# Gate products with the values as the stationary operand, logits by token rows, in an attention and mixture-of-experts kernel

## The chip, the cores and the metric

The kernel runs on one core of one Trainium2 chip. The metric is the device time of one execution in microseconds (us), the median of several runs of the whole kernel. Engines are named as in the profile: PE (TensorE, the matrix engine; PEld are its loads of a stationary operand), DVE (VectorE), ACT (ScalarE), POOL (GpSimd) and SP (the engine whose queue issues most transfers).

## The reference

Attention with a threshold over 8 batches of 8 heads (576 tokens, head size 64), then a router that gives every token to one of 8 experts with a fixed capacity of 576 tokens, then each expert's two-layer network. The change concerns one line of it, the gate product `logits = x @ w_gate`.

```python
scores = q @ k.T / 8                                  # each of 8 x 8 heads, 576 x 576
scores = where(scores >= max(scores) - tau, scores, -1e9)
attn = exp(scores - max(scores)); attn /= sum(attn) + 1e-9
x = (attn @ v), heads side by side                    # 4608 tokens x 512
logits = x @ w_gate                                   # 4608 x 8
# all 4608 * 8 logits in falling order: a token goes to the first expert that still has room
out[tokens of e] = relu(x[tokens of e] @ w1[e]) @ w2[e]
```

## The kernel before

The program has two stages. Attention for all batches comes first; the router and the experts come behind it. The change lies in the attention stage and its last few microseconds.

**Tiles and passes.** A batch has 4 pairs of heads, a pair has 9 tiles of score rows (eight of 128 rows, and the last, number 8, with the remaining 64 rows of both heads), so there are 288 tiles. The main loop at the end of `attention` takes two tiles a pass, 144 passes, 18 to a batch. A tile goes through several passes: its scores on PE (`score`, L69), in the next passes the negated minimum and a copy on DVE (`mx`, L74), the threshold on POOL (L75), the exponential on ACT (`ex`, L86), the masked product with its row sum on DVE (`stt`, L90), eight transposes of 64x64 pieces on PE (`tr`, through `turn`, L98) and their eviction by ACT (`trev`, L116 and L118). The products with the values (`pv_unit`, L155, and `pl_unit`, L165, for the last 64 keys) stand in a list, `queue`, with due passes, and `columns` takes from it. Their outputs collect in two PSUM banks (`xo`, one for columns 0 to 255 of the tokens and one for 256 to 575), are evicted by ACT at L145 and form `XT[b]`: for each of the four head pairs a tile of 128 partitions (two heads of 64) by 576 tokens, not yet divided by the row sums. `RD[b]` holds the reciprocals of the sums, `Lg` the logits by token rows.

**Order.** Every engine works in the order in which the program is written. In one pass PE gets: scores of two tiles, the transposes of leftover pieces where a tile 8 is near (`left`; such passes are called p8, four of every nine), what `columns` takes, one unit from `side` unless the pass is p8, and the transposes of two older tiles. Evictions noted in `later` are issued by ACT in the next pass (`flush`).

**The score tile.** A tile of scores uses columns 0 to 287 of two PSUM banks. Columns 288 to 511 are free; `free(t)` gives them to other work, the leftover transposes and the side units.

**The gate.** When the last product of a batch is evicted, `finish(b)` appends two units to `aux` and two to the front of `side`. Those of `aux` run in the next two passes, also in p8 ones, when the second `xo` bank is free (`whole`): `lg_unit` multiplies with the gate weights as the stationary operand (L177: four head pairs, 128x32, in four column strips of the array, moving the 256 or 320 token columns of `XT`), and ACT evicts the result into `LT` (L179). Those of `side` run in the next passes that are not p8: `lgt_unit` transposes three, then two, blocks of 128 token columns of `LT` (L202 through `turn`, L98, in the timeline `sc<-ident,lt`), ACT evicts them into `lw` (L219), and POOL multiplies with the reciprocals and adds up heads (L223 to L231). The second of them also copies the reciprocals of the last 64 tokens across partitions (`both`, L185 on PE, L188 on ACT). The last 64 tokens of an even and of the following odd batch share a column of `Lg`; an odd batch puts them into partitions 64 to 127.

For batches 0 and 1 `side` then holds ten units of row transposes of `XT` (`xt_early`), which end in stores of rows to memory; later batches do these behind the loop. The last batch does its gate work in `tail`, behind the loop: `lg_mm` and `lg_ev` for both column ranges, `lgt_mm`, and the sums on DVE (`logits`, L208 and L210), which the router needs first.

The two places where a pass takes its units:

```python
if sc_: columns(); whole()
ready=[x for x in side if x[0]()]
if ready and not p8: side.remove(ready[0]); ready[0][1](sc_[-1])
```

Of the kernel before, what the change touches and what calls it, by code (L numbers as in the profile page):

```python
# [19 lines left out]
PPB=8; LTB=1; VTB=4; HOLD=1; XW=520; NBO=2; NDEF=4; XTB=4; XTY=1.05; XT0=2.0; XRB=2  # L20


def attention(ctx, tc, qk, vl, tau, wgd, xrows, xts, Lg, nb_batches, ident, dup, R, after_first):
# [143 lines left out]
    RD={}  # L167
# [4 lines left out]
    LT={}; lt6=cst.tile([128,D],F32,name="lt6")  # L172
    def lg_mm(b,f,ps):
        if f==0: LT[b]=wk.tile([128,S+D],F32,name="lt",bufs=LTB)
        q=FQ[f]; n=q.stop-q.start
        for j in range(4):
            T.matmul(ps[32*j:32*j+32,:n],wg[:,j],XT[b][:,j,q],start=True,stop=True,tile_position=(0,32*j))  # L177
    def lg_ev(b,f,ps):
        q=FQ[f]; n=q.stop-q.start; c=0 if f else HEAD(b); A.activation(LT[b][:,c:c+n],ps[:,:n],AF.Copy)  # L179
    def HEAD(b): return S-256+(D if b==nb_batches-1 else 0)  # L180
# [9 lines left out]
    def lg_unit(b,f):  # L190
        ps=bank_v([128,512],1)
        lg_mm(b,f,ps)
        def ev():
            lg_ev(b,f,ps)
            if f==1:
                if b==nb_batches-2: G.tensor_scalar(lt6,LT[b][:,256:320],1.0,0.0,op0=ALU.mult,op1=ALU.add)
                have["lt"]=b
        return ev
    def lgt_mm(b,c0,c1,ps):
        for c in range(c0,c1):  # L200
            a=HEAD(b)+128*c if c<2 else 128*c-256 if c<4 else 192 if b%2 and b<nb_batches-1 else 256
            turn(ps[:,:,64*(c-c0):64*(c-c0)+64],LT[b][:,a:a+128])  # L202
    def lgt_in(ps,n): return ps[:,:,0:64*n].rearrange("p r (m k) -> p r m k",k=32)[:,:,:,0:16]
    def logits(b,c0,c1,ps,o):
        n=c1-c0; w=wk.tile([128,320],F32,name="lw",bufs=1)[:,0:64*n].rearrange("p (c j r h e) -> p c j r h e",c=n,j=2,r=2,h=2)
        lv=lgt_in(ps,n)
        for r in range(2):
            V.tensor_tensor(w[:,:,:,r].rearrange("p c j h e -> p (c j) h e"),lv[:,r].rearrange("p m (h e) -> p m h e",h=2),  # L208
                RD[b][:,r,c0:c1].rearrange("p c j h -> p (c j) h").unsqueeze(3).to_broadcast([128,2*n,2,8]),op=ALU.mult)
        V.tensor_reduce(Lg[:,o:o+n,:],w.rearrange("p c j r h e -> p c e (j r h)"),axis=AX.X,op=ALU.add)  # L210
    LW={}
    def lgt_unit(b,half,t):
        n=5 if b<nb_batches-2 else 4
        c0,c1=((0,3),(3,n))[half]; y=free(t)
        lgt_mm(b,c0,c1,y)
        if half: both(b,y[:,:,128:])
        else: LW[b]=wk.tile([128,320],F32,name="lw",bufs=1).rearrange("p (r c j h e) -> p r c j h e",r=2,c=5,j=2,h=2)
        w=LW[b]
        A.activation(w[:,:,c0:c1].rearrange("p r c j h e -> p r (c j) (h e)"),lgt_in(y,c1-c0),AF.Copy)  # L219
        if half: both_ev(b,y[:,:,128:],slice(0,128),A)  # L220
        for r in range(2):
            v=w[:,r,c0:c1].rearrange("p c j h e -> p (c j h) e")
            G.tensor_tensor(v,v,RD[b][:,r,c0:c1].rearrange("p c j h -> p (c j h)").unsqueeze(2).to_broadcast([128,4*(c1-c0),8]),op=ALU.mult)  # L223
        v=w[:,:,c0:c1]
        G.tensor_tensor(v[:,0],v[:,0],v[:,1],op=ALU.add)
        G.tensor_tensor(v[:,0,:,0],v[:,0,:,0],v[:,0,:,1],op=ALU.add)
        m=min(c1,4)-c0
        G.tensor_tensor(Lg[:,4*b+c0:4*b+c0+m,:],v[:,0,0:m,0,0],v[:,0,0:m,0,1],op=ALU.add)
        if c1==5:
            r=slice(64*(b%2),64*(b%2)+64)  # L230
            G.tensor_tensor(Lg[r,28+b//2,:],w[r,0,4,0,0],w[r,0,4,0,1],op=ALU.add)  # L231
    XR={}
    def xt_early(b,c,i,t):
# [5 lines left out]
        if i==0: G.tensor_scalar(xr[:n,512:XW].rearrange("p (r k) -> p r k",r=2),RD[b][:n,:,c].rearrange("p r j h -> p r (j h)"),1.0,0.0,op0=ALU.mult,op1=ALU.add)  # L239
# [103 lines left out]
    for s_ in range(-2,NT//2-2):  # L343
# [16 lines left out]
        for t in sc_: mx(t)  # L360
# [653 lines left out]
```

## Time and profile before

| | |
|---|---|
| median of 3 runs | 979.26 us (976.64 to 979.54) |
| the profiled execution | 973.59 us, its span 971.8 us |
| attention stage, main loop | from 5.5 us to about 439 us of the span |
| granted PE clock | 0.990 of full speed over the span |
| PE, gate products L177 | 128 records, 418 ns mean, 11.4 us busy in all |
| PE, transposes of logits | 78 records, 243 ns mean, 5.8 us busy in all |
| ACT, evictions L179 and L219 | 16 and 14, 6.3 and 4.1 us |
| POOL, L223 to L231 | 76 operations, 23.7 us |

In rows of the profile `out<-in` are the program's names of tiles, then come partitions x elements and the count. A PE row has the part of the array that it uses (rows*columns) ahead of the operand. Busy time of a group is the union of its records; records of PE overlap, so the mean of one record is longer than its share. A window `a:b` is a stretch of the span in us.

### The profile page before, as it was taken

To read this page: it belongs to the slowest core of one execution; us is meant where nothing else is said; L and a number is where in the kernel's file an instruction comes from. 1 tells how busy PE (TensorE), PEld (TensorE's weight loads), DVE (VectorE), ACT (ScalarE), POOL (GpSimd) and SP (SyncE) were. 2 spreads that over 40 slices of the span, in tenths; PEclk is the share of its full clock that TensorE was granted. 3 is DMA by queue.
4 is the path that set the end of the run, shared out by engine and by line. 5 is a ranking of instruction groups with operands and counts; after the bars stand their busy time and mean duration, and the time that the engine had idled before them with its cause. 6 is when DMAs were issued, how large, how long until landed. Compare 5 with 4: busy or idle time off the path is not lost.

```text
span 971.8 us, 24280 instructions
## 1 busy us (share of the span) xinstructions
PE 943.4 (97%) x9235; PEld 704.5 (72%) x9235; DVE 764.0 (79%) x2086; ACT 639.3 (66%) x1297; POOL 279.8 (29%) x493
## 2 busy tenths in 40 slices
PE   7999999999999999998789999999999999999996
PEld 4566656566566665565678797897978979898994
DVE  8999999999999999996679888586887786535220
ACT  6999999999999999996554344342543425445330
POOL 2435354353434343340110403222203022310202
PEclk9999999999999999999889999999999999999998
DMA  7332253533432333206742525151524344431101
GB/s 257 103 119 88 85 184 102 200 129 110 168 116 93 123 110 113 87 2 226 263 131 95 173 98 154 56 187 58 178 79 142 120 138 140 137 120 38 39 12 44
DMA packets 35860, 117.01 MB, mean 120 GB/s; under 512 B 4384, under 2 KB 5024, under 8 KB 35232
## 3 DMA queue, kind: packets, MB, share of 16 engines
q1 hardware_dynamic: 28352, 92.85, 27.8%
q0 software_dynamic: 5888, 19.03, 6.3%
q10 hardware_dynamic: 1504, 3.59, 1.2%
q8 instruction: 73, 1.20, 0.5%
q14 instruction: 43, 0.35, 0.1%
HBM read 93.01 MB, written 21.38 MB: 118 GB/s over the span
## 4 chain that ended last, share of the span: by engine, by line
PE 89%; DVE 5%; DMA 3%; issue 2%; ACT 1%; POOLq 0%; SPq 0%; ACTq 0%; DVEq 0%
PE pf L844 22%; PE pf L876 20%; PE sc L69 15%; PE xo L155 14%; PE tb L98 8%; PE sc L98 2%; PE pt L789 2%; PE xo L165 2%; DVE pp L90 1%; PE rps L497 1%; DVE z L74 1%; DVE cmp L426 1%; PE xo L177 1%; PE xo L246 1%; DMA out_dram<-y,idx 1%
## 5 line engine op out<-in xcount | busy, mean ns | idle before, releaser
L74 DVE TENSOR_SCALAR_CACHE_REDUCE z<-sc 128x576 f32<-128x576 f32 x288 | 206.1, 752 | 16.9 <-PE sc L69 15.0
L75 POOL TENSOR_SCALAR nb<-nb,taub 128x1 f32<-128x1 f32 x288 | 144.9, 504 | 249.9 <-DVE z L74 187.3
L86 ACT ACTIVATE pp<-z,nb 128x576 f32<-128x576 f32 x256 | 193.1, 773 | 26.0 <-DVE z L74 22.7
L90 DVE SCALAR_TENSOR_TENSOR pp<-z,nb,pp 128x576 f32<-128x576 f32 x256 | 200.0, 813 | 0.0
L876 PE MATMUL pf<-w2h,H 128*128 128x512 f32 x576 | 193.9, 401 | 0.8 <-DVE H L426 0.8
L69 PE MATMUL sc<-qk 64*128 64x288 f32 (+1 forms) x1280 | 179.9, 426 | 0.9 <-DMA qk<-qk_dram 0.4
L155 PE MATMUL xo<-pt,vt 128*64 128x320 f32 (+1 forms) x1024 | 155.9, 420 | 0.0
L116 ACT ACTIVATE pt<-tb 128x512 f32<-128x512 f32 x253 | 137.5, 590 | 2.0 <-PE tb L98 1.4
L883 POOL DMA_INDIRECT out_dram<-y,idx x40 | 44.6, 1114 | 307.2 <-ACT y L879 198.3
L876 PE MATMUL pf<-w2l,H 128*128 128x512 f32 x320 | 128.9, 403 | 0.0
L876 PEld LDWEIGHTS pf<-w2h,H 128*128 128x128 f32 x576 | 106.5, 188 | 20.3 <-DVE H L426 1.3
L69 PEld LDWEIGHTS sc<-qk 64*128 64x128 f32 (+1 forms) x1280 | 94.3, 179 | 28.7 <-DVE z L74 4.0
L844 PE MATMUL pf<-xh,w1h 128*128 128x288 f32 (+2 forms) x512 | 110.3, 301 | 0.7 <-ACT xh L790 0.7
L844 PE MATMUL pf<-xl,w1h 128*128 128x288 f32 (+2 forms) x512 | 110.4, 302 | 0.0
L844 PE MATMUL pf<-xh,w1l 128*128 128x288 f32 (+2 forms) x512 | 109.5, 299 | 0.0
L879 ACT ACTIVATE y<-pf 128x512 f32<-128x512 f32 x40 | 23.9, 598 | 128.8 <-PE pf L876 127.5
L98 PEld LDWEIGHTS tb<-ident,pp 64*128 64x128 f32 x2032 | 75.2, 139 | 44.7 <-issue 18.9
L155 PEld LDWEIGHTS xo<-pt,vt 128*64 128x64 f32 x1024 | 60.7, 136 | 58.5 <-issue 32.4
L856 ACT ACTIVATE hf<-pf 128x576 f32<-128x576 f32 x56 | 36.5, 652 | 89.3 <-PE pf L844 82.5
L98 PE MATMUL tb<-ident,pp 64*128 64x64 f32 x2032 | 91.8, 227 | 3.3 <-ACT pt L116 3.0
L844 PEld LDWEIGHTS pf<-xh,w1h 128*128 128x128 f32 x512 | 82.1, 190 | 1.6 <-ACT xh L790 1.1
L844 PEld LDWEIGHTS pf<-xh,w1l 128*128 128x128 f32 x512 | 81.9, 189 | 0.1
(197 smaller groups left out, 1334.7 us busy)
## 6 DMA issues: line engine op xcount, KB each, us to landing
qk<-qk_dram SPq DMA_DIRECT2D x31, 864.0 KB, 4.6
vt<-vl_dram SPq DMA_DIRECT2D x32, 576.0 KB, 4.0
w2s<-w_dram SPq DMA_DIRECT2D x32, 512.0 KB, 4.9
w1s<-w_dram SPq DMA_DIRECT2D x28, 512.0 KB, 5.3
xrows<-pp SPq DMA_DIRECT2D x24, 260.0 KB, 2.4
xts<-xt SPq DMA_DIRECT2D x2, 1152.0 KB, 5.4
pt<-xts SPq DMA_DIRECT2D x2, 1152.0 KB, 5.2
xrows<-xr SPq DMA_DIRECT2D x8, 260.0 KB, 2.5
```

The costliest lines, as they stand in the source:

```text
L69: T.matmul(sc[o,f,:HS], kd["q",h][r,c], kd["k",h][r,:],start=True,stop=True)
L74: V.tensor_scalar(z,SC.pop(t)[:,:,:HS],-0.125,None,op0=ALU.mult,op1=ALU.min,accum_out=nb[:,0:1])
L75: G.tensor_scalar(nb[:,1:2],nb[:,0:1],taub[:,0:1],None,op0=ALU.add)
L86: A.activation(pview(t),ZB[t].rearrange("p a b -> p (a b)"),AF.Exp,bias=NBI[t][:,0:1],scale=-1.0)
L90: V.scalar_tensor_tensor(pv,ZB.pop(t).rearrange("p a b -> p (a b)"),NBI[t][:,1:2],pv,op0=ALU.is_le,op1=ALU.mult,accum_out=den_of(p)[:,p%4/ ...
L98: g=slice(64*r,64*r+64); T.transpose(o[:,r],x[r%len(x)][g],ident[g,g])
L116: else: A.activation(o,tb,AF.Copy)
L155: T.matmul(xo[64*h:64*h+64,:q.stop-q.start],v[:,f,128*u+64*h:128*u+64*h+64],PT[p][:,h,u,q],start=new,stop=last,skip_group_check=True)
L844: T.matmul(ps[:,h,:n],s[w][:,k,f*128:(f+1)*128],s[x][:,k,cols[h]],start=(i==0),stop=(i==11))
L856: A.activation(hf,ps[:,:,:HS],AF.Relu)
L876: T.matmul(ps[:,0,:],H[:,f,c:c+128],s[w][:,f],start=(f==0 and j==0),stop=e)
L883: G.indirect_dma_start(out=out,out_offset=IOA(ap=s["idx"][:n,t:t+1],axis=0),in_=y[:n],in_offset=None)
```

## The change

The stationary and the moving operand of the gate product change places. A 128x64 piece of `XT` (one head pair, 64 tokens) is loaded, and the 16 gate columns of that pair move through it: the result has tokens in partitions and is what the transposes made before. Two such pieces, for the lower and the upper 64 tokens of a chunk of 128, use the two column halves of the array. The gate units no longer use an `xo` bank, `LT`, `lg_unit`, `lgt_unit` and `whole` go, and a batch has three units in `side`: chunks 0 and 1, chunks 2 and 3, chunk 4 with `both`. POOL's operations of these units and the small copies of `xt_early` go into a list, `small`, from which each pass issues two; a row store first issues all that are left. In the tail the two products of the last batch become `gate(b,0,2,z)` and `gate(b,2,5,x)`.

```diff
+    def gate(b,c0,c1,ps):
         for c in range(c0,c1):
+            for j in range(4):
+                for a in range(2):
+                    x,q=(b,128*c+64*a) if c<4 else (b-a*(b==nb_batches-1),512)
+                    o=32*(c-c0)+16*(j%2)
+                    T.matmul(ps[64*a:64*a+64,j//2,o:o+16],XT[x][:,j,q:q+64],wg[:,j,0:16],start=True,stop=True)
+    def gate_in(ps,n): return ps[:,:,0:32*n].rearrange("p r (m e) -> p r m e",e=8)
...
-    LW={}
-    def lgt_unit(b,half,t):
+    LW={}; small=[]
+    def do_small(n):
+        for _ in range(min(n,len(small))): small.pop(0)()
+    def gate_unit(b,i,t):
         n=5 if b<nb_batches-2 else 4
-        c0,c1=((0,3),(3,n))[half]; y=free(t)
-        lgt_mm(b,c0,c1,y)
-        if half: both(b,y[:,:,128:])
+        c0,c1=2*i,min(2*i+2,n); m=c1-c0; y=free(t)
+        if m: gate(b,c0,c1,y)
+        if i==2: both(b,y[:,:,128:])
...
+        if m: A.activation(w[:,:,c0:c1].rearrange("p r c j h e -> p r (c j h) e"),gate_in(y,m),AF.Copy)
+        if i==2: both_ev(b,y[:,:,128:],slice(0,128),A)
+        if not m: return
+        v=w[:,:,c0:c1]; u=v.rearrange("p r c j h e -> p r (c j h) e")
+        small.append(lambda: G.tensor_tensor(u,u,RD[b][:,:,c0:c1]...,op=ALU.mult))
+        small.append(lambda: G.tensor_tensor(v[:,0],v[:,0],v[:,1],op=ALU.add))
+        small.append(lambda: G.tensor_tensor(v[:,0,:,0],v[:,0,:,0],v[:,0,:,1],op=ALU.add))
...
+        small.append(lambda: G.tensor_tensor(Lg[r,o:o+m,:],v[r,0,:,0,0],v[r,0,:,0,1],op=ALU.add))
...
     def finish(b):
-        aux.extend([lambda: lg_unit(b,0),lambda: lg_unit(b,1)])
-        side[:0]=[(lambda: have.get("lt")==b,lambda t,i=i: lgt_unit(b,i,t)) for i in range(2)]
+        side[:0]=[lambda t,i=i: gate_unit(b,i,t) for i in range(3)]
...
         x=wide(); z=wide()
-        lg_mm(b,0,x[:,0]); both(b,z[:,:,256:]); lg_ev(b,0,x[:,0])
+        gate(b,0,2,z); both(b,z[:,:,256:])
         both_ev(b,z[:,:,256:],slice(0,64),V); V.tensor_copy(rd[64:128,:,4],RD[b-1][64:128,:,4])
+        logits(b,0,2,z,31); R.prep(31,33)
         for u in range(1,4): pv_unit(p,1,u,False)
         close(1); flush()
-        lgt_mm(b,0,2,z)
-        lg_mm(b,1,x[:,1]); G.tensor_scalar(LT[b][:,320:384],lt6,1.0,0.0,op0=ALU.mult,op1=ALU.add)
-        logits(b,0,2,z,31); R.prep(31,33)
-        lg_ev(b,1,x[:,1])
-        lgt_mm(b,2,5,z[:,:,264:]); logits(b,2,5,z[:,:,264:],33)
+        gate(b,2,5,x); logits(b,2,5,x,33)
...
         for t in sc_: mx(t)
+        do_small(2)
...
-        if sc_: columns(); whole()
-        ready=[x for x in side if x[0]()]
-        if ready and not p8: side.remove(ready[0]); ready[0][1](sc_[-1])
+        if sc_: columns()
+        if side and not p8: side.pop(0)(sc_[-1])
```

The first place is PE's order in four passes of the main loop, from the second of the two passes with L177 of batch 0 (numbers of buffers left out; `sc` is a score tile or its free columns, `tb` the bank of the tile transposes). Before:

```order
L155 MATMUL xo_1272<-pt,vt 64x256 x4
L177 MATMUL xo_1335<-xt,wg 32x320 x4
L98 MATMUL tb<-ident,pp 128x64 x16
L69 MATMUL sc<-qk 128x288 x2
L69 MATMUL sc<-qk 64x288 x4
L165 MATMUL xo_1272<-pl,vt 64x256 x2
L165 MATMUL xo_1386<-pl,vt 64x320 x2
L155 MATMUL xo_1386<-pt,vt 64x320 x2
L98 MATMUL sc<-ident,lt 128x64 x6
L98 MATMUL tb<-ident,pp 128x64 x16
L69 MATMUL sc<-qk 128x288 x4
L155 MATMUL xo_1386<-pt,vt 64x320 x4
```

The same place after, where L188 is the new product:

```order
L155 MATMUL xo_1271<-pt,vt 64x256 x4
L98 MATMUL tb<-ident,pp 128x64 x16
L69 MATMUL sc<-qk 128x288 x2
L69 MATMUL sc<-qk 64x288 x4
L165 MATMUL xo_1271<-pl,vt 64x256 x2
L165 MATMUL xo_1372<-pl,vt 64x320 x2
L155 MATMUL xo_1372<-pt,vt 64x320 x2
L188 MATMUL sc<-wg,xt 64x16 x16
L98 MATMUL tb<-ident,pp 128x64 x16
L69 MATMUL sc<-qk 128x288 x4
L155 MATMUL xo_1372<-pt,vt 64x320 x4
L188 MATMUL sc<-wg,xt 64x16 x16
```

L177 is gone from the p8 passes (the one of 256 columns, a pass earlier, too), and two units of 16 products stand where six and four transposes of logits stood. The third unit, on PE three passes later, after:

```order
L155 MATMUL xo_1506<-pt,vt 64x256 x2
L155 MATMUL xo_1605<-pt,vt 64x320 x2
L188 MATMUL sc<-wg,xt 64x16 x8
L176 MATMUL sc<-rd,dup 128x4 x2
L98 MATMUL tb<-ident,pp 128x64 x16
```

L176 is `both`, L185 before; it stood behind the second unit and stands behind the third, which is a pass that held a row transpose of batch 0 before. The second place is POOL's order over the same passes, where L75 is the threshold of each tile. Before, and then after:

```order
L75 TENSOR_SCALAR nb<-nb,taub 128x1 x14
L223 TENSOR_TENSOR lw<-lw,rd 128x96 x2
L225 TENSOR_TENSOR lw<-lw 128x96
L226 TENSOR_TENSOR lw<-lw 128x3x16
L228 TENSOR_TENSOR Lg<-lw 128x24
L75 TENSOR_SCALAR nb<-nb,taub 128x1 x2
L223 TENSOR_TENSOR lw<-lw,rd 128x64 x2
```

```order
L75 TENSOR_SCALAR nb<-nb,taub 128x1 x16
L211 TENSOR_TENSOR lw<-lw,rd 128x2x64
L212 TENSOR_TENSOR lw<-lw 128x64
L75 TENSOR_SCALAR nb<-nb,taub 128x1 x2
L213 TENSOR_TENSOR lw<-lw 128x2x16
L216 TENSOR_TENSOR Lg<-lw 128x16
L75 TENSOR_SCALAR nb<-nb,taub 128x1 x2
```

The sums of one unit stood in one run ahead of the next pass's L75; they now come two at a time, each two behind a pass's L75. The third place is PE's order in the tail. Before, and then after:

```order
L177 MATMUL sc<-xt,wg 32x256 x4
L185 MATMUL sc<-rd,dup 128x4 x2
L155 MATMUL xo_7553<-pt,vt 64x320 x6
L165 MATMUL xo_7553<-pl,vt 64x320 x2
L98 MATMUL sc<-ident,lt 128x64 x4
L177 MATMUL sc<-xt,wg 32x320 x4
L98 MATMUL sc<-ident,lt 128x64 x6
```

```order
L188 MATMUL sc<-wg,xt 64x16 x16
L176 MATMUL sc<-rd,dup 128x4 x2
L155 MATMUL xo_7674<-pt,vt 64x320 x6
L165 MATMUL xo_7674<-pl,vt 64x320 x2
L188 MATMUL sc<-wg,xt 64x16 x24
```

The second product with its eviction and the transposes behind it are one run of 24 products now.

More of the change, by code (lines that the diff above doesn't have):

```diff
@@ L218, in lgt_unit @@
         w=LW[b]
[L219 to L226, printed above, removed]
@@ L252, in xt_unit @@
         return ev
-    queue=[]; aux=[]; side=[]; later=[]; late=[]; late2=[]; st={"last":-9,"slot":0}
+    queue=[]; side=[]; later=[]; late=[]; late2=[]; st={"last":-9,"slot":0}
     def push_pair(p):
```

52 lines of the change are left out of this document (14 added, 38 removed).

## The prediction

> **What bounds the kernel now.** I read first the page's busy times and its forty slices.
>
> ```profile
> PE 943.4 (97%) x9235; PEld 704.5 (72%) x9235; DVE 764.0 (79%) x2086; ACT 639.3 (66%) x1297; POOL 279.8 (29%) x493
> PE   7999999999999999998789999999999999999996
> DVE  8999999999999999996679888586887786535220
> ```
>
> The change lies in the attention stage, which fills the first 18 slices (24.3 us each, to about 440 us). PE and DVE are both full there, so shares cannot tell which of them sets the pace. A table of windows can. Below, one window is one pass of the main loop (two tiles, from the DVE's first L74 of the pass to that of the next); after the window come its length and the busy time of PE, weight loads, DVE, ACT and POOL. The first four rows are passes without gate work. The next four stand at the same places of a later batch, where the gate work is done; the last two are the fifth and sixth pass counted from the start of that work.
>
> ```profile
> 321.38:324.24 2.86, 2.86 (x40) 2.01 (x38) 2.86 (x11) 2.71 (x6) 0.97 (x2) 1.00 0.54 185
> 324.24:327.08 2.84, 2.84 (x40) 1.73 (x40) 2.84 (x9) 2.82 (x8) 1.07 (x2) 1.00 0.03 6
> 327.08:330.09 3.01, 3.01 (x42) 1.73 (x40) 2.92 (x10) 3.01 (x8) 0.97 (x2) 1.00 0.43 103
> 330.09:332.99 2.90, 2.90 (x34) 1.66 (x32) 2.90 (x8) 2.56 (x6) 0.97 (x2) 1.00 0.47 198
> ...
> 347.78:350.93 3.15, 3.15 (x46) 2.01 (x44) 2.93 (x11) 3.06 (x7) 0.97 (x2) 1.00 0.42 150
> 350.93:354.40 3.47, 3.47 (x48) 1.84 (x48) 2.92 (x8) 3.44 (x9) 1.07 (x2) 1.00 0.02 5
> 354.40:357.64 3.24, 3.24 (x48) 1.96 (x50) 2.92 (x8) 3.12 (x8) 1.54 (x4) 1.00 0.47 137
> 357.64:360.89 3.25, 3.25 (x42) 2.02 (x40) 2.93 (x8) 2.85 (x8) 2.77 (x8) 1.00 0.34 136
> ...
> 366.70:369.54 2.84, 2.84 (x36) 1.49 (x36) 2.84 (x11) 2.84 (x7) 1.07 (x2) 1.00 0.00 0
> 369.54:372.50 2.96, 2.96 (x42) 1.68 (x36) 2.91 (x10) 2.72 (x7) 0.97 (x2) 1.00 0.42 100
> ```
>
> Two things are to be seen. No pass is shorter than about 2.84 us, and in those that are just as long DVE is busy throughout: two L74 and two L90 are the floor. And the four gate passes take 13.11 us where the same four without gate work take 11.61, with PE busy for their whole length and DVE not. The timeline shows the other side of it: ahead of the first L74 of a pass, DVE stood idle for PE's scores (in brackets).
>
> ```profile
> 354.40 0.76 DVE L74 TENSOR_SCALAR_CACHE_REDUCE z<-sc 128x576 f32<-128x576 f32 x1 [0.56 <-PE sc L69]
> 357.64 0.76 DVE L74 TENSOR_SCALAR_CACHE_REDUCE z<-sc 128x576 f32<-128x576 f32 x1 [0.32 <-PE sc L69]
> ```
>
> Last, the chain of waits over this batch (start, length, what). It runs on PE alone and prices the gate work by what it adds:
>
> ```profile
> 349.12 0.57 PE xo L177 x8
> ...
> 352.49 0.68 PE xo L177 x8
> ...
> 356.22 0.33 PE sc L98 x5
> ...
> 359.31 0.27 PE sc L98 x4
> 359.57 0.17 PE sc L185 x4
> ```
>
> So in a gate pass **PE sets the time**, and the first four rows, 1.85 us per batch, are what the change takes out; L185 stays. It is worth less than 1.85: without L177 the first two passes would be those at 321 and 324, and nothing goes below the DVE's 2.84.
>
> **What the new products cost.** A batch issues 5 chunks x 4 head pairs x 2 halves = 40 products, each with 64 stationary and 16 moving columns. A product in f32 leaves two records of each kind: L177 has 8 products in each of 7 batches and 112 records. So there are 80 loads and 80 short matmuls a batch. The two halves go to different columns of the array, as in L155, so they form 40 pairs, each a load and a matmul of both halves. Nothing of this shape is in the trace; the nearest rows are these.
>
> ```profile
> L177 PE MATMUL xo<-xt,wg 128*32 128x256 f32 (+1 forms) x112 | 9.7, 418 | 0.0
> 349.05 0.64 PE L177 MATMUL xo<-xt,wg 128*32 128x256 f32 x8
> L155 PEld LDWEIGHTS xo<-pt,vt 128*64 128x64 f32 x1024 | 60.7, 136 | 58.5 <-issue 32.4 <-ACT pt L118 0.4
> 355.46 0.20 PEld L155 LDWEIGHTS xo<-pt,vt 128*64 128x64 f32 x4 [0.48 <-issue]
> 356.33 0.58 PEld L98 LDWEIGHTS tb<-ident,pp 64*128 64x128 f32 x16
> 359.35 0.31 PEld L185 LDWEIGHTS sc<-rd,dup 64*128 64x128 f32 x4
> 454.33 0.33 PE L503 MATMUL sc<-cn,eyer 128*32 128x8 f32 x4
> ```
>
> L155 loads the stationary operand of the new products: 128x64 in f32, halves alternating. Four loads took 0.20 us and one takes 0.136, so the second pair began at most 0.064 us behind the first, and the halves load side by side. L185's loads are twice as wide, and its second pair came about 0.31 - 0.19 = 0.12 behind: a load goes by its columns. The moving side is short: in the L177 row the second records stand 0.64 - 0.42 = 0.22 us behind the first for 256 columns, so 16 columns are about 0.014. L98, eight pairs of loads and short transposes in 0.58, shows that such a stream keeps its pace: (0.58 - 0.14) / 7 = 0.063 a pair. I take **0.060 us a pair**, between L155 and the bare load. The near ends are 0.055 (load alone) and 0.073 (load, then stream). The far ends are 0.031, the pace of L503, whose four products of 32 stationary columns follow each other about every (0.33 - 0.17 - 0.06) / 3 us, with 0.17 for the last record and 0.06 for the first load; and 0.12, if the two halves load in turn.
>
> By the Trainium skill, "TensorE: Matmul & The Clock Gate", section "LDWEIGHTS (loading the stationary operand)", a load costs its columns over 1.2 GHz whatever its rows: an estimate of 53 ns for 64, which L155's row bears out; by it alone 40 pairs would be 2.1 us. The Trainium skill, "TensorEngine Tiling (Array Packing)", section "Instruction Overhead", also speaks against this change: it has a matmul of one moving column cost as much as one of 60 and warns against tiling on a side that is already small. No row here has 16 moving columns in f32, so the trace cannot yet say.
>
> **Where they stand.** 40 pairs are 2.4 us of PE time in place of 1.85, and in other passes: none in the first two, 16 pairs (0.96) in the third and in the fourth, and 8 pairs (0.48) with L185 in the fifth, because passes with leftover transposes take no side unit. What such a pass becomes, these rows show (third pass):
>
> ```profile
> 355.09 0.75 DVE L74 TENSOR_SCALAR_CACHE_REDUCE z<-sc 128x576 f32<-128x576 f32 x1
> 355.46 0.76 PE L155 MATMUL xo<-pt,vt 128*64 128x320 f32 x4
> 356.15 0.26 PEld L98 LDWEIGHTS sc<-ident,lt 64*128 64x128 f32 x6 [0.49 <-DVE z L74]
> ```
>
> The unit writes free columns of the score tile that the second L74 reads, and waits for it, as the old transposes did. That L74 ends at 355.84, 1.44 us into the pass. Behind the unit come the tile transposes (356.33 in the row above), then the scores; from there to the next first L74 at 357.64 it is 1.31. Between L155's products, which end near 356.05 (0.06 of load and twice 0.27, the 0.22 scaled to 320 columns), and the 356.15 of the next kind lie 0.09 of changeover. The plain pass at 330 is then 1.50 + 0.09 + 1.31 = 2.90, which is its row. The new products have L155's array shape and need no changeover ahead of them; the one behind them was there before. They cannot start before 1.44 plus a handoff of some 0.06, however early PE is, so the lead that PE gains in the first two passes is of little use. Hence:
>
> - passes 1 and 2: 2.84 each, DVE's floor (before 3.15 and 3.47);
> - passes 3 and 4: 2.90 + 0.96 = 3.86 each (before 3.24 and 3.25);
> - pass 5: 2.90 + 0.48 + 0.17 = 3.55 (before 2.84);
> - pass 6: the row's 2.96 and about 0.09, a lead it had from pass 5 and has no more: 3.05.
>
> Together 20.00 against 18.91: **+1.09 us a batch**, 6.5 for batches 0 to 5. Batch 6 has four chunks: pass 5 is 2.90 + 0.17, some +0.6. Batches 0 and 1 have row transposes in side units behind the gate; each moves on by one free pass, at no cost.
>
> **The other engines.** These rows price what else moves.
>
> ```profile
> L90 DVE SCALAR_TENSOR_TENSOR pp<-z,nb,pp 128x576 f32<-128x576 f32 x256 | 200.0, 813 | 0.0
> L179 ACT ACTIVATE lt<-xo 128x256 f32<-128x256 f32 (+1 forms) x14 | 5.5, 395 | 0.0
> L219 ACT ACTIVATE lw<-sc 128x192 f32<-128x192 f32 (+2 forms) x14 | 4.1, 295 | 0.0
> ```
>
> ACT loses two evictions of 0.395 and two of 0.295 per batch and gains three of the last kind, at most as large: 0.8 us less. ACT waits for PE in gate passes, so I count nothing; at the limit it is 0.8 a batch, were ACT the bound. Behind the eviction ACT's queue holds the next pass's evictions, whose transposes stand behind the same products on PE, so the later eviction holds up nothing new. POOL's multiplications and additions come two to a pass behind the two L75 instead of in one run; L90, which needs L75's result, never waited (0.0), and its busy 2.77 of 3.25 us eases: nothing. SP's stores of rows go one or a few passes later, and the first reader is the next stage: nothing.
>
> **The tail** (last batch, after the loop) has a chain of its own.
>
> ```profile
> 444.38 0.64 PE L177 MATMUL sc<-xt,wg 128*32 128x256 f32 x8
> 447.83 0.44 ACT L145 ACTIVATE xt<-xo 128x320 f32<-128x320 f32 x1 [2.28 <-PE xo L165]
> 449.08 0.44 ACT L179 ACTIVATE lt<-sc 128x320 f32<-128x320 f32 x1 [0.82 <-PE sc L177]
> 450.02 0.42 DVE L208 TENSOR_TENSOR lw<-sc,rd 128x96 f32<-128x96 f32 x2
> ```
>
> The first unit is 0.96 instead of 0.57, so all behind it moves by some 0.35. Behind the last L145 (448.27), 1.75 us pass now until L208: product, eviction, transposes. After the change, 18 pairs wait for that eviction, 1.08, and with 0.3 for the handoffs it is some 1.4. The two cancel: 0.
>
> **The sum** is 6.5 + 0.6 + 0 = +7.1. The profiled execution spans 971.8 us and took 973.59; it would take 980.7. The three runs lie higher (976.64 to 979.54, median 979.26); I put the same 7.1 on their median: **986.4 us**. With 272 exposed pairs in the loop, 0.055 takes 1.4 off and 0.073 adds 3.8 with the tail, 985.0 to 990.2, and a spread like that of the runs makes it 983.5 to 991.7.
>
> **Rivals.**
>
> - *The loads hide* (the one that is not slower): pairs at L503's 0.031. Then 272 x 0.029 = 7.9 and 0.6 in the tail go, and the gain of passes 1 and 2 outweighs the rest: 977.9. It decides below 0.034 a pair. For it: L503 has short f32 products this close. Against: its stationary side is half as wide, and L155 and L185 have loads go by width.
> - *The halves do not pair*: 0.12 a pair adds 272 x 0.06 = 16.3 and some 1.2 in the tail: 1003.9. For it: a matmul too short to cover the load of its neighbour. Against: L98 pairs at 0.063 with moving sides of 64. The Trainium skill, "TensorE: Matmul & The Clock Gate", section "The mechanism", has a load overlap running matmuls only in other rows of the array, and here all share the rows; L503, with shared rows, speaks against it.
>
> **Chances.** Forecast 0.79, hidden loads 0.13, no pairing 0.08. The range is 977 to 993: the forecast's own and the first rival; it leaves out the second. About 0.3% (2.9 us) is what a measurement can tell: below 976.3 is faster, 0.05, from the first rival's lower part; within, 0.12 (0.08 of it and 0.04 of the forecast); slower 0.83.
>
> **What would show it.** In the profile after, windows of a batch should read 2.84, 2.84, 3.86, 3.86, then 3.55 for the fifth; a unit of 16 products should take about 1 us of PE loads (32 loads in some 0.96 + 0.08); and L74's wait for PE should be gone from passes 1 and 2 and about 0.9 in 3 and 4. Wrong would be a unit under 0.55 or near 2 us, a DVE without waits in passes 3 to 5, or L90 waiting for POOL.

## The result, and the profile after

The changed kernel took 985.32 us, the median of 6 runs (983.14 to 987.17); the kernel before, on the same chip, took 978.85 us (976.64 to 980.89, 6 runs). The ratio is 1.0069, with a 95% interval of 1.0049 to 1.0089: slower by 0.7%. The forecast was 986.4 us, in a range of 977 to 993.

The profiled execution of the change took 983.14 us and spans 981.4 us. First the table of windows, pass by pass, for the batch that the prediction worked on (columns as there: window, length, busy time of PE, weight loads, DVE, ACT and POOL):

```profile
351.78:354.62 2.84, 2.84 (x40) 1.99 (x38) 2.84 (x11) 2.76 (x6) 0.97 (x2) 1.00 0.44 175
354.62:357.45 2.83, 2.83 (x42) 1.75 (x42) 2.83 (x9) 2.81 (x8) 1.07 (x2) 1.00 0.00 0
357.45:361.29 3.84, 3.84 (x74) 2.58 (x68) 2.92 (x11) 3.42 (x9) 0.97 (x2) 1.00 0.65 206
361.29:365.13 3.84, 3.84 (x66) 2.68 (x64) 2.92 (x8) 2.83 (x7) 2.15 (x4) 1.00 0.08 31
365.13:368.10 2.97, 2.97 (x40) 2.01 (x38) 2.92 (x8) 2.71 (x7) 1.71 (x3) 1.00 0.23 43
368.10:370.94 2.84, 2.84 (x39) 1.95 (x36) 2.84 (x7) 2.82 (x8) 1.87 (x5) 1.00 0.44 169
370.94:374.54 3.60, 3.60 (x56) 2.18 (x56) 2.92 (x11) 3.29 (x9) 2.65 (x6) 1.00 0.00 0
374.54:377.59 3.05, 3.05 (x42) 1.77 (x44) 2.92 (x8) 2.78 (x7) 1.73 (x3) 1.00 0.44 114
```

The first two passes sit on DVE's floor: the products L177 are gone from them. In the third and fourth, units of new products stand where the transposes of logits stood; these passes grew from 3.24 and 3.25 to 3.84, the pass with the third unit from 2.84 to 3.60, and in these three DVE is busy for 2.92 only and PE for the whole length. The fifth and sixth rows are passes without gate work, as long as before; the last two rows are the prediction's fifth and sixth pass. The chain of waits through the same stretch (start, length, what) and the timeline show the same from two other sides:

```profile
358.98 1.08 PE sc L188 x32
...
362.95 0.95 PE sc L188 x32
...
372.46 0.62 PE sc L188 x16
373.08 0.32 PE sc L176 x4
```

```profile
358.94 1.01 PEld L188 LDWEIGHTS sc<-wg,xt 128*64 128x64 f32 x32 [0.53 <-DVE z L74]
...
361.29 0.76 DVE L74 TENSOR_SCALAR_CACHE_REDUCE z<-sc 128x576 f32<-128x576 f32 x1 [0.92 <-PE sc L69]
```

On the chain the gate work of a batch was 0.57 + 0.68 + 0.33 + 0.27 + 0.17 us before and is 1.08 + 0.95 + 0.62 + 0.32 now, on PE alone. A unit of 16 products is 32 loads in 1.01 us, and DVE waits 0.92 us for the scores behind it. 32 loads are 16 pairs of halves; without the last load (0.138) a pair comes every (1.01 - 0.138) / 15 = **0.058 us**.

### The profile page after: what moved, and what is told of

The parts are those of the page before. It is cut to its first block, busy times and chain, and to the rows that moved or that the text cites. A ratio compares the mean times of both kernels' runs of the same rounds, so it can differ in the third digit from the quotient of the medians.

```text
span 981.4 us, 25094 instructions
## 1 busy us (share of the span) xinstructions
PE 950.4 (97%) x9653; PEld 718.6 (73%) x9653; DVE 762.6 (78%) x2086; ACT 637.3 (65%) x1287; POOL 295.2 (30%) x495
## 3 DMA queue, kind: packets, MB, share of 16 engines
q8 instruction: 76, 1.25, 0.5%
## 4 chain that ended last, share of the span: by engine, by line
PE 89%; DVE 5%; DMA 2%; issue 2%; ACT 1%; POOLq 0%; POOL 0%; SPq 0%; ACTq 0%; DVEq 0%
PE pf L824 22%; PE pf L856 19%; PE sc L69 14%; PE xo L155 14%; PE tb L98 8%; PE sc L188 2%; PE xo L165 2%; PE pt L769 2%; PE sc L98 2%; DVE z L74 1%; DVE pp L90 1%; PE rps L477 1%; DVE cmp L406 1%; PE xo L233 1%; DMA out_dram<-y,idx 1%
## 5 line engine op out<-in xcount | busy, mean ns | idle before, releaser
L74 DVE TENSOR_SCALAR_CACHE_REDUCE z<-sc 128x576 f32<-128x576 f32 x288 | 205.8, 751 | 23.3 <-PE sc L69 21.0
L75 POOL TENSOR_SCALAR nb<-nb,taub 128x1 f32<-128x1 f32 x288 | 145.4, 505 | 244.5 <-DVE z L74 192.1
L90 DVE SCALAR_TENSOR_TENSOR pp<-z,nb,pp 128x576 f32<-128x576 f32 x256 | 199.9, 813 | 0.0
L155 PE MATMUL xo<-pt,vt 128*64 128x320 f32 (+1 forms) x1024 | 155.9, 420 | 0.0
L98 PEld LDWEIGHTS tb<-ident,pp 64*128 64x128 f32 x2032 | 75.1, 139 | 40.9 <-issue 15.4
L155 PEld LDWEIGHTS xo<-pt,vt 128*64 128x64 f32 x1024 | 60.6, 136 | 58.5 <-issue 32.3
L98 PE MATMUL tb<-ident,pp 64*128 64x64 f32 x2032 | 92.2, 228 | 3.3 <-ACT pt L116 3.0
L824 PEld LDWEIGHTS pf<-xl,w1h 128*128 128x128 f32 x512 | 81.8, 190 | 1.5 <-issue 1.5
```

The lines of the kernel that those rows point to most:

```text
L74: V.tensor_scalar(z,SC.pop(t)[:,:,:HS],-0.125,None,op0=ALU.mult,op1=ALU.min,accum_out=nb[:,0:1])
L75: G.tensor_scalar(nb[:,1:2],nb[:,0:1],taub[:,0:1],None,op0=ALU.add)
L90: V.scalar_tensor_tensor(pv,ZB.pop(t).rearrange("p a b -> p (a b)"),NBI[t][:,1:2],pv,op0=ALU.is_le,op1=ALU.mult,accum_out=den_of(p)[:,p%4/ ...
L98: g=slice(64*r,64*r+64); T.transpose(o[:,r],x[r%len(x)][g],ident[g,g])
L155: T.matmul(xo[64*h:64*h+64,:q.stop-q.start],v[:,f,128*u+64*h:128*u+64*h+64],PT[p][:,h,u,q],start=new,stop=last,skip_group_check=True)
L824: T.matmul(ps[:,h,:n],s[w][:,k,f*128:(f+1)*128],s[x][:,k,cols[h]],start=(i==0),stop=(i==11))
```

## Experiments

Each kernel is the changed one with the edit shown. "Third", "fourth" and "third-unit pass" are the three passes of the batch around 360 us that hold gate work (3.84, 3.84 and 3.60 in the change). "The loop" is the time from the second pass's first L74 to that of the last, 142 passes: 433.15 us in the change, 426.85 in the kernel before. As x5 will show for the kernel before, it came out the same to 0.3 us in two executions, which the whole time did not; so one profile of each kernel was enough for most questions. The kernels of one group (x1 to x4; x5 to x8; x9 to x11) ran on one chip, each group on another.

### What a stationary load costs: x1 to x4

Theory W is the prediction's: a load takes as long as its columns are many, loads into different columns of the array run side by side, and this sets the pace. The other theories price the instruction, or have the pairing not matter. Four edits of the product loop, the last one of its caller:

```
# x1_wide: one 128-column load per product in place of two halves (chunks 0-3)
+ if c<4:
+     T.matmul(ps[:,j//2,o:o+16],XT[b][:,j,128*c:128*c+128],wg[:,j,0:16],...); continue
# x2_strip: four strips of 32 columns
- for a in range(2): ... XT[x][:,j,q:q+64]
+ for a in range(4): T.matmul(ps[32*a:32*a+32,j//2,o:o+16],XT[x][:,j,q:q+32],wg[:,j,0:16],...,tile_position=(0,32*a))
# x3_nopair: the same products, all of one half of a chunk first
- for j in range(4):
-     for a in range(2):
+ for a in range(2):
+     for j in range(4):
# x4_double: every product twice
- if m: gate(b,c0,c1,y)
+ if m: gate(b,c0,c1,y); gate(b,c0,c1,y)
```

> The new product with chunks 0 to 3 as one 128x128 stationary piece instead of two 128x64 halves (chunk 4 unchanged): half the instructions, loads twice as wide. In the changed kernel a pair of halves costs 0.058 us. Theory W (a load costs its columns, and column parts of the array load side by side): 0.11 us for each piece and pass over it, a unit of two chunks 1.8 us instead of 0.93, third and fourth pass about 4.7 us instead of 3.84; about 12 us slower than the changed kernel in all. Theory I (the pace is set by the number of instructions, 0.0146 us each): 0.029 a piece, a unit 0.47, those passes 3.4; about 6 us faster than the changed kernel.

> The new product in four 128x32 strips instead of two 128x64 halves: twice the instructions, loads half as wide. Theory W (a load costs its columns, parts side by side): 0.03 us for the four strips and one pass over the operand, a unit 0.48 us instead of 0.93, third and fourth pass 3.4; about 7 us faster than the changed kernel, level with the kernel before. Theory I (0.0146 us an instruction): 0.117, a unit 1.9 us, those passes 4.8; about 15 us slower.

> The same products in another order: in each chunk first the four of the lower half, then the four of the upper, so that neighbours load the same column half. Theory W: a load waits for the one ahead of it in its half, 0.055 to 0.06 us each, a unit 1.8 us instead of 0.93, passes 3 and 4 about 4.7; about 15 us slower than the changed kernel. Theory I: the number of instructions is the same and nothing changes (within 0.1 us a pass).

> Every gate unit of the main loop issues its products twice into the same place (the tail once). If PE time of the products is fully on the path, as the forecast has it: passes 3 and 4 3.84 + 0.93 = 4.77 us each, the fifth 3.59 + 0.47 = 4.06, passes 1 and 2 stay at 2.84; 2.33 us a batch, some 16 us in all over the changed kernel. Rival (the passes are long because of the new wait for the second L74 or of ACT, and the products partly hide): clearly less, under 1.2 us a batch.

Measured, one execution each beside 973.81 us for the kernel before: x1 998.08, x2 979.75, x3 987.09, x4 998.31 us. The timelines of the weight loads have the row of the third pass's unit; below, in this order, those of x1, x2, x3 and x4 (start, length, what, count):

```profile
369.54 1.86 PEld L187 LDWEIGHTS sc<-wg,xt 128*128 128x128 f32 x16 [0.53 <-DVE z L74]
```
```profile
358.51 0.64 PEld L188 LDWEIGHTS sc<-wg,xt 128*32 128x32 f32 x64 [0.53 <-DVE z L74]
```
```profile
364.75 1.32 PEld L188 LDWEIGHTS sc<-wg,xt 128*64 128x64 f32 x32 [0.53 <-DVE z L74]
```
```profile
371.93 1.95 PEld L188 LDWEIGHTS sc<-wg,xt 128*64 128x64 f32 x64 [0.53 <-DVE z L74]
```

The same operand of 128 tokens costs, per record of 128 rows: 0.11 us as one piece (1.86 less the last load's 0.19, the mean of that group, over 15), 0.058 as two halves, 0.034 as four strips ((0.64 - 0.11) / 63 x 4). Half the instructions are twice as slow, and twice the instructions are faster: this is W, and a price per instruction is out. The passes follow. Here are the windows of the third and fourth pass of x1 and of x2:

```profile
368.05:372.73 4.68, 4.68 (x58) 3.42 (x52) 2.91 (x11) 3.41 (x9) 0.97 (x2) 1.00 0.58 193
372.73:377.52 4.79, 4.79 (x50) 3.52 (x48) 2.93 (x9) 2.83 (x7) 2.14 (x4) 1.00 0.00 2
```
```profile
357.02:360.48 3.46, 3.46 (x106) 2.21 (x100) 2.92 (x10) 3.41 (x9) 0.97 (x2) 1.00 0.61 198
360.48:364.04 3.56, 3.56 (x98) 2.30 (x96) 2.92 (x8) 2.85 (x7) 2.12 (x4) 1.00 0.16 63
```

With x1 the loop is 446.39, with x2 430.81, with x4 449.32 us. For x1 and x4 that is what W expected (13 and 16 us above the change). For x2 it is a miss: 7 us below the change were expected and 2.3 came. Three single passes account for 3.0 of the missing 4.7: its 46th, 64th and 100th pass take 4.39, 4.68 and 4.58 us where the fourth pass of its other batches takes 3.56; x8 comes back to them. x4's third and fourth pass are 4.77 and 4.78, 0.94 above the change's for 16 more pairs, again 0.058 each. So in a pass that holds a unit, all of its pairs are on the path, the first 16 as well as the next.

x3 missed what I expected of W. Its passes are 4.14 and 4.15 and its loop 439.27, 6 us above the change and not 15. Products of one half in a row do cost more, but 0.038 us a record ((1.32 - 0.138) / 31), not 0.058. Record by record the trace showed why that could be: inside a half the loads start 0.058 us apart, and around each change from one half to the other they interleave. x9 tests that.

### How far two halves overlap: x9

```
# x9_halves: all products of the unit for the first half, then all for the second
- for c in range(c0,c1):
-     for j in range(4):
-         for a in range(2):
+ for a in range(2):
+     for c in range(c0,c1):
+         for j in range(4):
```

> The change, but the 16 products of a unit (32 records) go all for the first half of the array and then all for the second, where x3 changed the half after every 8 records. Theory Q (each half of the array takes its loads one behind the other, 0.058 us each, and a record of the other half can start only a few places ahead of its turn): in x3 a unit of 32 records took 1.21 us, 31 steps of 0.058 less 0.2 for each of its three borders between halves; with one border it takes 31 x 0.058 - 0.2 = 1.6 us, the third and fourth pass 4.55 (x3 4.15), the fifth 3.85 as in x3, the loop 444 to 445 us (x3 439.3, the change 433.2). Rival R (a record finds its half free however far behind it stands): 0.93 us a unit and a loop of 433. Rival M (0.039 us is simply the price of a record when its neighbour is in the same half): 1.21 us a unit, passes of 4.15, a loop of 439.

The unit in the third pass of x9, and the third, fourth and third-unit pass:

```profile
368.62 1.73 PEld L188 LDWEIGHTS sc<-wg,xt 128*64 128x64 f32 x32 [0.53 <-DVE z L74]
```
```profile
367.13:371.69 4.56, 4.56 (x74) 3.30 (x68) 2.92 (x11) 3.43 (x9) 0.97 (x2) 1.00 0.62 199
371.69:376.26 4.57, 4.57 (x66) 3.40 (x64) 2.93 (x9) 2.83 (x7) 2.14 (x4) 1.00 0.00 0
382.06:385.91 3.85, 3.85 (x56) 2.43 (x56) 2.92 (x10) 3.27 (x9) 2.65 (x6) 1.00 0.00 0
```

Its loop is 445.08 us. All four numbers are theory Q's (1.73 less the last load's 0.138 is 1.6; 4.55, 3.85, 444 to 445), and far from R's and M's. Record by record, the loads of the first half start 0.058 us apart to the end, and the first load of the second half starts ahead of the last three of them. So each half takes its loads one behind the other, and a load for the other half started ahead of its turn by three places. The order of the program decides how much of this is used: with alternating halves the two loads of every pair start within 0.01 us of each other.

### The stage behind the loop: x5

The profile of the change was longer than that of before by 9.6 us of span (981.4 - 971.8), the loop by only 6.3. The stage behind the last logits, where both kernels run the same program, was longer by 4.0 (and the start of the program shorter by 0.7). x5 is the kernel before, unchanged, profiled once more.

> The kernel before, profiled once more, to see how much the stage behind the main loop (the same program in both kernels) differs from one execution to the next. Theory S (the 4.0 us by which that stage was longer in the profile of the change are scatter between executions): this execution takes 976 to 980 us, its main loop is as long as in the first profile of the kernel before to 0.3 us, and the stage behind it is 2 to 5 us longer than there. Rival C (the change lengthens that stage, by where its rows and sums come out): the stage is as long as in the first profile to 1 us, and the execution takes about 974 us.

It took 977.1 us. Two windows of each kernel, the loop and all that follows the last logits: first those of the kernel before, then x5's, then the change's.

```profile
8.23:435.08 426.85, 423.00 (x5334) 256.00 (x5336) 412.80 (x1152) 401.99 (x804) 176.27 (x386) 1.00 0.35 120
450.20:971.80 521.60, 500.08 (x3715) 437.13 (x3713) 336.85 (x880) 226.24 (x472) 100.56 (x96) 0.98 0.36 118
```
```profile
7.91:434.48 426.57, 422.35 (x5334) 255.55 (x5334) 412.80 (x1150) 402.28 (x804) 176.97 (x386) 1.00 0.35 121
449.60:975.30 525.70, 501.38 (x3715) 436.71 (x3713) 336.65 (x880) 226.44 (x472) 99.74 (x96) 0.98 0.36 117
```
```profile
7.58:440.73 433.15, 428.85 (x5698) 268.79 (x5698) 412.05 (x1150) 400.96 (x797) 192.35 (x389) 1.00 0.35 119
455.75:981.30 525.55, 501.74 (x3715) 437.05 (x3713) 336.37 (x880) 226.40 (x472) 100.60 (x96) 0.98 0.36 117
```

The loops of the two executions of the kernel before differ by 0.28 us, their last stage by 4.1; the change's last stage is as long as x5's to 0.15. That is theory S's outcome and not C's. But over all kernels of this study the stage took 521.5 (x3) to 529.0 us (x10), in no order that goes with the edits, and in one that goes with the chips: 521.5 to 524.7 in x1 to x4, 525.7 to 528.3 in x5 to x8, 527.6 to 529.0 in x9 to x11. So x5 alone does not tell scatter between executions from a difference between chips. The medians speak against C: by six runs of each kernel on one chip they differ by 6.5 us, as much as the loop alone; a last stage 4 us longer each time would make it 10. Scatter on one chip is there too: 17 executions of the kernel before, on the chip of x5, took 975.94 to 982.91 us. The change's own effect is its loop: 433.15 against 426.57 and 426.85, **+6.3 to 6.6 us**.

### The waits around the unit: x6, x7, x10

```
# x6_first: the unit uses the free columns of the pass's first score tile
- if side and not p8: side.pop(0)(sc_[-1])
+ if side and not p8: side.pop(0)(sc_)        # gate_unit: y=free(t[0]); xt_early: y=free(t[-1])
# x7_early: unit 0 is entered earlier in the batch, units 1 and 2 where they were
+ if j==3: queue.append(("n",lambda: True,False,lambda: later.append(([True],lambda: side.insert(0,lambda t: gate_unit(b,0,t)))),p))
- side[:0]=[lambda t,i=i: gate_unit(b,i,t) for i in range(3)]
+ side[:0]=[lambda t,i=i: gate_unit(b,i,t) for i in range(1,3)]
# x10_once: POOL does all waiting sums in one run
- do_small(2)
+ do_small(99)
```

> The change, but the gate unit writes the free columns of the pass's first score tile in place of those of the second, so it waits for the first L74 and no longer for the second. Theory W (PE stands still before the unit only where it comes to a gate pass with a lead): in the third and fifth pass of a batch PE's last L155 makes room at 358.81 and 372.30 and the products start at 358.94 and 372.44, so these passes get shorter by 0.13 and 0.14 (3.84 to 3.71, 3.59 to 3.45); the fourth has no lead and stays 3.85. In all 0.27 a batch, 1.6 to 1.9 us in the loop. Rival H (the lead lost is the 0.3 us by which PE was ahead in the passes before): 0.3 in each of these two passes, some 4 us. Rival N: the wait is taken over by another one, no change.

x6 took 983.21 us, with a loop of 430.78: 2.4 us less than the change, between W and H. The third, fourth and third-unit pass, and the unit of the third:

```profile
356.32:359.96 3.64, 3.64 (x74) 2.66 (x68) 2.92 (x10) 3.41 (x9) 0.97 (x2) 1.00 0.64 194
359.96:363.75 3.79, 3.79 (x66) 2.77 (x64) 2.93 (x9) 2.85 (x7) 2.15 (x4) 1.00 0.13 53
369.56:372.95 3.39, 3.39 (x56) 2.26 (x56) 2.92 (x10) 3.15 (x9) 2.66 (x6) 1.00 0.00 0
```
```profile
357.40 1.23 PEld L188 LDWEIGHTS sc<-wg,xt 128*64 128x64 f32 x32
```

Two passes give 0.20 each, and 0.05 comes from the fourth, which I had put at nothing. The step that I mis-sized: the loads of the unit no longer wait at all and the first start at 357.40, before L155's stream of that pass has ended (357.08 + 0.76), so the gain is more than the 0.13 in which PE had stood still. In three batches of seven the third pass gained nothing (3.89 as in the change). The wait for the second L74 is real, and it is worth 2.4 us of the 433.

> The change, but the first of the three gate units of a batch goes into an earlier pass of the batch before the leftover transposes, the others stay in order behind them. Theory W (PE is the bound of every pass with a unit, wherever it stands): the loop changes by less than 0.15 us a batch, under 1 us in all; the pass with the first unit takes about 3.85 wherever it stands. Rival P (the place matters, because some passes have PE time to spare under DVE's 2.84): over 0.4 us a batch shorter, 3 us in all.

x7 took 987.19 us, with a loop of 433.33, the change's to 0.2. Its windows at the first unit (now three passes earlier), at the second and third, and at the pass where the third had been:

```profile
350.20:354.03 3.83, 3.65 (x64) 2.67 (x64) 2.92 (x10) 3.23 (x8) 0.97 (x2) 1.00 0.62 199
...
359.74:363.64 3.90, 3.90 (x74) 2.81 (x72) 2.92 (x10) 3.44 (x9) 1.48 (x4) 1.00 0.58 190
363.64:367.24 3.60, 3.60 (x54) 2.44 (x52) 2.92 (x8) 2.83 (x8) 2.17 (x4) 1.00 0.12 45
373.06:375.90 2.84, 2.84 (x36) 1.50 (x36) 2.84 (x11) 2.84 (x7) 2.07 (x5) 1.00 0.00 0
```

The lengths moved with the units and the sum stayed: the pass that the first unit came into had, like those it came from, no PE time to spare under DVE's floor.

> The change, but POOL does all its waiting multiplications and additions of a unit in one run in the next pass, as the kernel before did, in place of two to a pass. By the prediction's step (POOL hides them behind L75, L90 never waits for it) the loop stays at 433.2 to 0.4 us and L90 has no idle time. Rival: one run of four is some 2 us on POOL, a later L75 and so L90 come late in that pass, 0.3 us or more for each of 20 units, 6 us in all.

x10's loop is 433.16 us, and L90 had no idle time. How POOL's small sums are spread costs nothing, as the prediction had it. (Its whole time, 986.41 us, is the longest last stage of the study, 529.0.)

### Can the products be made cheap enough: x8 and x11

x8 puts x2 and x6 together. x11 is x8 with one chunk to a unit:

```
# x11_strip5
- c0,c1=2*i,min(2*i+2,n)
+ c0,c1=i,min(i+1,n)
- side[:0]=[lambda t,i=i: gate_unit(b,i,t) for i in range(3)]
+ side[:0]=[lambda t,i=i: gate_unit(b,i,t) for i in range(5)]
...                                              # the last unit's index, 2, becomes 4
```

> Both improvements together: four strips of 32 columns per product in place of two halves, and the unit in the first score tile's free columns. By theory W the loop is about 4.8 us shorter from the strips (the first strip run was 19.27 a batch against 20.0, less its lone stalls of PE) and 1.7 from the earlier start: 979 us as the median of the runs where the change has 985.3, within 0.3% of the kernel before (ratio 0.998 to 1.003). Rival: PE's unexplained stalls of 0.6 to 0.8 us behind the units of 64 products grow with the earlier start, and it takes 983.

x8 took 983.21 us (12 runs), the ratio to the kernel before is 1.0045 (1.0030 to 1.0060). That is a miss: 979 was expected. Its loop is 429.91, where the expected sum comes to 426.7. Most passes are as short as W has them, but two in the loop are 4.7 us, 1.1 longer each than the fourth pass of the other batches. They are the 64th and the 100th pass, which are long in x2 too, though the two kernels ran on different chips, which suggests that the place in the program has a part in it. The first of them in x8, for comparison the third and fourth pass of the batch around 360 us, and the timeline on PE of the long one:

```profile
194.67:199.37 4.70, 4.07 (x101) 2.71 (x99) 2.92 (x9) 3.36 (x7) 2.14 (x4) 1.00 0.34 140
356.96:360.38 3.42, 3.42 (x106) 2.20 (x100) 2.92 (x10) 3.38 (x9) 0.97 (x2) 1.00 0.59 190
360.38:363.94 3.56, 3.56 (x98) 2.30 (x96) 2.92 (x8) 2.85 (x7) 2.12 (x4) 1.00 0.18 73
```
```profile
196.28 0.73 PE L188 MATMUL sc<-wg,xt 128*32 128x16 f32 x64
196.94 0.72 PE L98 MATMUL tb<-ident,pp 64*128 64x64 f32 x16
197.49 0.46 PE L69 MATMUL sc<-qk 64*128 64x288 f32 x1
198.58 0.99 PE L69 MATMUL sc<-qk 64*128 64x288 f32 x6 [0.63 <-issue]
```

PE stands still for 0.63 us in the middle of the scores, and "issue" says that no semaphore and no transfer of data is to be seen as its releaser. It begins 0.9 us behind a unit of 64 matmuls and 64 loads in 0.7 us. x8's other one and the three of x2 also fall within such a unit or in the microsecond behind it. x11 keeps the products and takes away the crowding.

> x8 (strips, unit in the first score tile) with five units of one chunk (32 records) in place of three of up to two (64 records). Theory F (PE's lone stalls of 0.6 to 0.9 us in x2 and x8 come because a unit of 64 short products uses up PE's instructions faster than they are fetched): the stalls are gone in the loop, the passes of 4.7 us are no more, and the loop is about 2.2 us shorter than x8's 429.9, some 427.7, against 426.6 in the kernel before; the median is then 980 to 981 and the ratio to the kernel before 1.000 to 1.003. Rival G (the stalls come from the number of instructions in all, which is the same): they stay, elsewhere, and the loop stays near 430. Rival A (two more evictions and eight more sums a batch cost): longer than x8.

x11 took 982.59 us (12 runs), ratio 1.0029 (1.0013 to 1.0046), with a loop of 429.04. Its five unit passes:

```profile
355.62:358.75 3.13, 3.13 (x74) 1.92 (x68) 2.92 (x10) 3.13 (x9) 0.97 (x2) 1.00 0.58 172
358.76:362.03 3.27, 3.27 (x66) 2.01 (x64) 2.93 (x9) 2.65 (x7) 1.84 (x4) 1.00 0.27 106
367.84:370.97 3.13, 3.13 (x68) 1.75 (x68) 2.92 (x10) 3.08 (x8) 2.28 (x6) 1.00 0.02 5
370.97:374.40 3.43, 3.43 (x74) 2.12 (x76) 2.93 (x9) 3.04 (x8) 2.13 (x5) 1.00 0.46 145
374.40:377.89 3.49, 3.49 (x70) 2.24 (x68) 2.92 (x8) 3.08 (x9) 1.94 (x4) 1.00 0.51 166
```

The lone stalls of 0.6 to 0.9 us are gone from the loop, and no gate pass is longer than 3.5 us. With the same number of products in all, that is theory F's outcome and not G's, in one profile of each kernel. One is left, in the tail, where the second gate product is not cut into units and has 96 records in a run (x11's timeline of PE):

```profile
452.33 0.59 PE L188 MATMUL sc<-wg,xt 128*32 128x16 f32 x46 [0.99 <-issue]
```

The tails of x2 and x8, with the same run, have one each (0.67 and 0.44 us).

The likely reading is that PE waited for its instructions, and the transfers bear it out. Queue q8 moves 16 KB at a time, of the kind `instruction`; here is the one ahead of x8's stall, from the view of the transfers in the window 196:197.3 (packets, MB, share of 16 engines):

```profile
q8 instruction: 1, 0.02, 4.8%
```

It lands at 197.24, and PE goes on at 198.58, 1.34 us later. In all eight stalls of x2, x8 and x11, tails included, the resuming instruction starts 1.25 to 1.51 us behind such a landing, though the stalls last 0.44 to 0.99 us. Mostly these transfers come every 10 us or so (the median in the change is 9.7); around each of the eight stalls two of them start 3.3 to 4.3 us apart. No other idle time of PE's matmuls over 0.15 us is put down to "issue" between 20 and 460 us of the thirteen profiles. But pairs as close as these also pass without a stall (all four of x4, with its 64 loads of 64 columns in 1.95 us), and no edit moved the fetch alone; so the fetch as the cause is strongly suggested, not shown.

The loop did not fall to 427.7: a batch's five passes take 16.45 us where x8's same five, 3.42 + 3.56 + 3.35 + 3.06 + 2.90, take 16.29, so spreading costs 0.16 in this batch; over the whole loop it takes back 1.4 of the 2.2 us that the two stalls had cost x8. No version beat the kernel before; x11, the nearest, is 0.3% slower.

## Why the prediction was right

**Which engine sets the time.** Right. x1 to x4 and x9 change nothing but PE's products (their width, number or order), and the loop follows each of them.

**The price of a pair.** 0.060 us was forecast and 0.058 measured. The two rivals fell with it: pairs at 0.031 are what four strips give (0.034 in x2), and 0.12 is what a load of the full width gives (0.11 in x1). The prediction took both numbers from rows with these numbers of columns (L503 and L185), and chose the row with the right one, L155. The rival "the halves do not pair" was not only wrong for this order of the products: even x3 and x9, which keep the halves apart, come to 0.038 and 0.05 a record. Inside one half their loads start 0.058 us apart, which is that rival's price; the mean is lower because loads around a border between halves interleave.

One of the rows that the prediction leaned on does not carry it. L98's pairs, at 0.063, were to show that a stream of loads keeps the pace of 64 columns. But its loads are 128 columns wide by their row, as L185's are, whose pairs came 0.12 apart: the mean load takes 0.139 us in L98 and 0.192 in L185. So the transposes do not follow the price by columns, and that their pace lies near 0.060 was luck. L98 is a transpose and L185 is not; whether that is why was not tried. The forecast stands without that row: L155's row bounds the pair at 0.064.

**The passes.** Forecast 2.84, 2.84, 3.86, 3.86, 3.55 and 3.05; measured 2.84, 2.83, 3.84, 3.84, 3.60 and 3.05. The fifth's 0.05 more goes with L176, which stands on the chain with 0.32 us where L185 had 0.17; that it is the cause was not tried. What the first two passes gain is as said: not more than down to DVE's floor.

**The sum of the loop.** Forecast +7.1, measured +6.3 to 6.6. Counted over 18 passes from a batch's first gate pass, batches 2 to 5 come to 1.05 to 1.18 each (forecast 1.09) and batch 6 to 0.56 (forecast 0.6). Batches 0 and 1, whose side units also hold row transposes, come to 0.91 and 0.70: the prediction used one batch's sum for all six, and the 0.6 us too much is there. The passes show where. In batch 0 the pass of the third unit held a row transpose before, so it was 2.92 long and not 2.84, and the pass behind it did not grow (3.18 in both kernels). In batch 1 it is much the same (2.89; 3.15 to 3.18), and its first gate pass, which came behind row transposes of batch 0, fell from 3.44 to 2.87 where that of batch 0 fell from 3.14 to 2.84 (batch 2's fell as far, but its later passes grew by 0.3 in all). That the row transposes are the cause was not tried.

**The lead that PE gains is of little use**, because the unit waits for the second L74. Right in sign, and x6 gives its size: with the unit waiting for the first L74 instead, 2.4 us come back.

**Tail, ACT, POOL and SP: nothing.** The tail from the last pass to the last logits is 15.12 us before and 15.02 after. ACT's evictions of the gate work fell by 0.63 us a batch (9.66 to 5.24 us over the seven batches; 0.8 was forecast). L90, which would have to wait for POOL, has no idle time, in the change and in x10.

**The profiled execution.** The sum was put on the span of one execution, 980.7, and on the median of the runs. The median was met (985.32 against 986.4). The execution, at 983.14, was not, by 2.4 us, which is the 4.0 us by which the last stage was longer, less 0.8 of the loop, 0.7 at the start of the program and 0.1 in the tail.

## What to carry to other kernels

Where short products follow each other, price them by the columns of their stationary operand, and look in the profile for a row of the same operation with that very width. Here a record of 128 tokens cost 0.11, 0.058 or 0.034 us as one, two or four pieces, with 16 moving columns throughout; longer moving sides were not tried, and transposes did not follow this price. Cut into column parts that alternate, the same operand loads in parallel, and wide pieces or runs of one part give that away. And to compare two kernels of which one stage is unchanged, compare the changed stage alone: here the loop repeated to 0.3 us in two executions, while the stage behind it differed by 4.1 in them and by 7.5 over all profiles.

## What the runs showed of the hardware that was not expected

- Loads for the other half of the array start ahead of their turn, by three places in x9: from the first load's start to the last's, a unit of 32 takes 0.87 us where the halves alternate, 1.18 with three borders (x3), 1.59 with one (x9).
- A dense run of short products can be followed by a stall of PE, within it or up to a microsecond later, of 0.6 to 0.9 us: in the loop only with 64 records of 32 columns in a unit (x2, x8; five of 28 such units), not with 32 (x11) and not with 64 records of 64 columns (x4); 1.0 us in x11's run of 96 in the tail. Each of these stalls ended 1.25 to 1.51 us behind the landing of 16 KB of instructions.
- POOL's small operations took longer or shorter by their neighbour, as the profile records them (its spans on POOL are rough). The addition of 32 columns took 0.74 us where it comes directly behind an L75 (mean of 14 in the change), and 0.25 behind another addition (mean of 20 in x10, six of them of 16 columns). The first fence is the change's timeline of POOL, the second x10's:

```profile
366.67 0.79 POOL L75 TENSOR_SCALAR nb<-nb,taub 128x1 f32<-128x1 f32 x1 [0.39 <-DVE z L74]
367.43 0.74 POOL L213 TENSOR_TENSOR lw<-lw 128x32 f32<-128x32 f32 x1
```
```profile
364.47 0.32 POOL L212 TENSOR_TENSOR lw<-lw 128x64 f32<-128x64 f32 x1
364.86 0.26 POOL L213 TENSOR_TENSOR lw<-lw 128x32 f32<-128x32 f32 x1
```

  Two sums at a time in place of one run went with a POOL busy time in the loop of 192.4 us against 184.5 (x10), with no effect on the loop's length (433.15 and 433.16).
